# A fused attention and gated-MLP block: side tiles as single matmuls over the whole array, and a head ordered by traced load times

## The chip, the cores and the metric

One core of one Trainium2 chip. The metric is the device time of one launch in microseconds; the time of a kernel is the median of its runs. The engines are TensorE (matmul, weight load), VectorE, ScalarE, GpSimd and SyncE, which issues the DMAs.

## The reference

```python
x = A_x                                   # (1, 2048, 512), bf16
xn = layernorm(x)                         # no scale, no shift
q, k, v = split(xn @ wqkv)                # 32 heads of 16 columns
o = softmax(q @ k.T * 16 ** -0.5) @ v     # over all 2048 keys, for each head
h = silu(xn @ w1) * (xn @ w3)             # 1792 columns
return x + o @ wo + h @ w2
```

## The kernel before

The 2048 tokens are 16 token tiles of 128. The 32 heads are 8 groups of 4, so that the 4 heads of a group sit in the four strips of 32 partitions. A *unit* is a group and a block of queries (256 as a rule, 128 in the first two units and at the end).

Each score is computed twice. **Pass one** (line 1008) multiplies 128 queries by 512 keys for two heads at a time, in two strips of 32 rows of TensorE's array, and VectorE takes the row maxima of the two banks (line 1048, a TENSOR_REDUCE of 128x1024). Of these there are 1024. The maximum of a row goes, negated, into spare rows of the transposed queries (lines 1133 and 1135, and either a small matmul tile named AQ, or a DMA transpose). **Pass two** (line 1272) computes the scores again, keys on the partitions and the maximum already subtracted, and ScalarE takes the exponential into `PT` (line 1285, or 1315 for two banks at once). The tile named PV multiplies `PT` with the values and a column of ones; the sums of the ones are inverted on GpSimd and multiplied in by way of DMAs.

Everything else of TensorE is a **side tile** in a bank of its own: the K and Q of the first group straight into `KT` and `QT` (`tile_KT`, `tile_QT`), the others in `tile_heads` by way of a DRAM buffer, `tile_V`, the gate and up projections (`ffn_pair`, `G` and `U`), the output tiles (`tile_OUT`, `tile_OUTA`, `tile_OUTB`) and AQ. All of these and PV go through `col_groups` (line 564), which splits each product into four matmuls of 32 stationary columns, side by side in the four column strips of the array:

```python
for i in range(n):
    ins = e.matmul(bank(bk)[32 * i:32 * i + m, c0 + a:c0 + b], make_lhsT(i),
                   rhs if (a, b) == (0, ncols) else rhs[:, a:b],
                   start=start, stop=stop, tile_position=(0, 32 * i), **kw)
```

**The head.** SyncE loads `x` in five pieces, the weights between and behind them (`LOADS`). For each token tile: statistics on VectorE (line 593) or, for two groups of tiles, on ScalarE (583 and 587); coefficients on GpSimd (606, and the power at 609); the normalisation itself (line 626) on the engine that a letter of `NORM` names for its group, `d` VectorE, `p` GpSimd, `a` ScalarE (line 622); four transposes on TensorE (650); an eviction into `xnT` on ScalarE (657). When four token tiles are there, a K tile gives 512 keys of the first group.

```python
LN_GROUPS = ((0, 2), (2, 4), (4, 6), (6, 8), (8, 12), (12, 14), (14, 16))
NORM = "ddddppa"
```

In the first microseconds TensorE also runs **spare matmuls** on a tile of ones (`warm_cand`), later on `ident` and `xnT` (`fill_cand`), whose results nobody reads: they are there to keep TensorE's clock up.

**The order.** The order of each engine is written out when the program is built: a planner goes through all engines, with costs in microseconds for each instruction (`_c_mm`, `_c_act`, `_c_dve`), the landing times of the loads (`DMA_FIRST`, `DMA_RATE`), the costs of a change between row and column strips on TensorE (`pe_start`), and a running measure of how many columns TensorE has streamed lately (`note_load`), and picks for each engine the instruction that can start first. The chip then runs these fixed orders, with semaphores between the engines.

Of the kernel before, what the change touches and what calls it, by code (L numbers as in the profile page):

```python
# [14 lines left out]
_VIS = {"dve": 0.138, "pool": 0.085}  # L15

# [20 lines left out]
class _Prog:  # L37
# [87 lines left out]
    def pe_start(self, mode, groups, ready):  # L125
        t = max(self.free["pe"], ready)
        if mode == "col":
            t = max(t, max(self.rg) + (0.092 if self.pe_mode == "row" else 0.0))
        else:
            t = max(t, max(self.rg[g] for g in groups))  # L130
            if self.pe_mode == "col":
                t = max(t, max(self.rg) + 0.106)
        return t

    def pe(self, fn, reads, writes, mode, groups, dur, name="", first=None):
# [11 lines left out]
        for g in (range(4) if mode == "col" else groups):  # L147
            self.rg[g] = start + dur
        if mode == "row" and self.pe_mode == "col":
            for g in range(4):  # L150
                self.rg[g] = max(self.rg[g], start)
# [64 lines left out]
class _Tile:  # L216
    __slots__ = ("groups", "evac", "name", "bank", "pred", "need", "on_start", "paced", "cols")
# [29 lines left out]
def _build(nc, A_x, A_wqkv, A_wo, B_w1, B_w3, B_w2, out):  # L247
# [36 lines left out]
    DMA_FIRST = 3.25  # L284
# [34 lines left out]
    NORM = "ddddppa"  # L319
# [25 lines left out]
    with ctx:  # L345
# [134 lines left out]
        landed = [DMA_FIRST]  # L480

        def load(fn, keys, kb):
            landed[0] += kb / DMA_RATE
# [6 lines left out]
        def load_w(dst, keys, off, n=D):  # L490
            load(lambda e: e.dma_start(dst, wqkv_v[:, :, off * D:off * D + n]), keys, n if n == D else 280)
# [81 lines left out]

        def ln_chunk(gi):
# [43 lines left out]
            def norm(op):  # L618
                for t in tl:
# [11 lines left out]
                    else:  # L631
                        poolq["nx"].append(_Item(*it, 0.7, 0.8, **kw))
# [50 lines left out]
        def tile_heads(what, g0, ng, sc, need):  # L683
# [4 lines left out]
            def grp(c):  # L688
                return lambda bk: col_groups(bk, lambda i: w[:, c, 64 * g0 + 32 * i:64 * g0 + 32 * i + 32],
                                             lambda i: xnT[:, c, sc * 512:(sc + 1) * 512], 512,  # L690
                                             start=c == 0, stop=c == DC - 1, n=2 * ng)
# [43 lines left out]
        def tile_V(t, need=None):  # L735
            groups = []
            for c in range(DC):
                groups.append((lambda bk, c=c: col_groups(
                    bk, lambda i: xnT[:, c, t * 128 + 32 * i:t * 128 + 32 * i + 32], lambda i: wv[:, c, :], D,
# [12 lines left out]
        def qt_groups(qc, g, q0, nq, stop_last):  # L752
            groups = []
            for c in range(DC):
                groups.append((lambda bk, c=c: col_groups(
                    bk, lambda i: wpad["q", g][:, c, 32 * i:32 * i + 32],
                    lambda i: xnT[:, c, qc * 512 + q0:qc * 512 + q0 + nq], nq,
# [12 lines left out]
        def tile_QT2(u):  # L770
# [4 lines left out]
            for qt in range(nq // 128):  # L775
                groups.append((lambda bk, qt=qt: col_groups(
                    bk, lambda i: Z[:, par, qt, 32 * i:32 * i + 32], lambda i: ident[:, :], 128, c0=qt * 128,
                    start=False, stop=True, skip=True),
# [17 lines left out]
        def ffn_pair(sc, fc):  # L796
# [19 lines left out]
            def groups(which):  # L816
                return [(lambda bk, c=c: col_groups(
                    bk, lambda i: w13[:, sl, which * DC + c, 32 * i:32 * i + 32],
                    lambda i: xnT[:, c, sc * 512:(sc + 1) * 512], 512, start=c == 0, stop=c == DC - 1),
# [36 lines left out]
        def g_x(tg, stop=False):  # L856
            return (lambda bk: col_groups(bk, lambda i: ident[:, 32 * i:32 * i + 32], lambda i: xr[:, tg % NXR, :], D,
                                          start=True, stop=False),
                    [("ident",), ("xr", tg % NXR)], _c_mm(512), None)

        def g_h(tg, fc, stop=False):
            qc, ts = divmod(tg, 4)
            hs = hslot(qc * FC + fc)
            return (lambda bk: col_groups(bk, lambda i: hT[:, hs, ts * 128 + 32 * i:ts * 128 + 32 * i + 32],
                                          lambda i: w2[:, fc, :], D, start=False, stop=stop),
                    [("hT", hs), ("w2",)], _c_mm(512), None)

        def g_on(qc, ts, g, start, stop):
            ob = (qc + 1) % 2
            return (lambda bk: col_groups(bk, lambda i: onorm[ob][:, g, ts * 128 + 32 * i:ts * 128 + 32 * i + 32],  # L870
                                          lambda i: wo[:, g, :], D, start=start, stop=stop),
# [671 lines left out]
        def col_cand():  # L1543
            best = None
            for t in sorted(active, key=rank):
# [9 lines left out]
                st = P.pe_start("col", None, P.ready("pe", reads, writes))  # L1555
# [8 lines left out]
            def emit_half():  # L1564
# [3 lines left out]
                P.pe(a, reads, writes, "col", None, _c_mm(256), name=t.name, first="act")  # L1568
# [4 lines left out]
            def emit():  # L1573
                g = t.groups.pop(0)
                P.pe(fn, reads, writes, "col", None, dur, name=t.name, first="act")
# [44 lines left out]
        def warm_cand():  # L1620
# [3 lines left out]
            for bk in (3, 2, 5, 4) if not p1_n[0] else (5, 4):  # L1624
# [3 lines left out]
                st = P.pe_start("col", None, P.ready("pe", [("ones_t",)], writes))  # L1628

                def emit():  # L1630
# [4 lines left out]
                return st, emit, _c_mm(128)  # L1635
            return None

        def fill_cand():
# [8 lines left out]
            for fb in fbs:  # L1647
                if fb in bank_tenant or fb in p2_busy:
                    continue
                s_ = P.pe_start("col", None, P.ready("pe", (), [("ps", fb)]))  # L1650
# [6 lines left out]
            def emit():  # L1657
                P.pe(col_groups(bk, lambda i: ident[:, 32 * i:32 * i + 32], lambda i: xnT[:, 0, 0:512], 512),
# [253 lines left out]
```

## Time and profile before

| | us |
|---|---|
| median of three runs | 1217.35 |
| the three runs | 1213.72, 1217.36, 1217.35 |
| the profiled execution | 1215.26 |
| its span, first to last instruction | 1213.5 |
| busy: VectorE, ScalarE, TensorE, GpSimd | 1180.8, 1168.3, 1155.1, 453.4 |
| mean granted clock of TensorE | 0.992 |

Matmuls are pipelined, so TensorE's busy time holds their latency as well and is no measure of how full it is. In the rows of a timeline stand the start, the time from the first start to the last end, the engine, the line, the operation, what it writes and reads, the count, and in brackets the idle time ahead of it and what ended that. "issue" is a wait for nothing that the profile shows. A row of windows has, for each engine in the order PE, PEld, DVE, ACT, POOL, the busy time and the count of instructions, then TensorE's granted clock, the share of the DMA engines and GB/s.

### The profile page before, as it was taken

What the parts mean: (1) busy time and instruction counts of PE and PEld (TensorE: products, weight loads), DVE (VectorE), ACT (ScalarE), POOL (GpSimd) and SP (SyncE); (2) the same over time, 40 slices, a digit from 0 to 9 for tenths busy, and PEclk for the clock granted to TensorE, in tenths of its full rate; (3) what the DMA queues carried; (4) which work ended last, traced back from release to release, by engine and by line L of the source; (5) the groups of instructions that cost most, each with busy time, mean ns of one, the idle gap of its engine ahead of it and who ended that gap; (6) DMA issues with size and microseconds to landing.
All of it is one profiled execution on the core that took longest, in us unless ns stands there. A gap on an engine that the chain in (4) does not pass through costs nothing.

```text
span 1213.5 us, 45673 instructions
## 1 busy us (share of the span) xinstructions
PE 1155.1 (95%) x20085; PEld 479.1 (39%) x20085; DVE 1180.8 (97%) x1083; ACT 1168.3 (96%) x2276; POOL 453.4 (37%) x862
## 2 busy tenths in 40 slices
PE   6999999999999999999999999999999999999998
PEld 4343333333333433333333433333333333345554
DVE  6799999999999999999999999999999999999995
ACT  5599999999999999999999999999999999999997
POOL 6315563553422256552221246552222225233220
PEclk9799999999999999999999999999999999999999
DMA  6322322222101122120101122210000111100000
GB/s 172 102 63 62 85 53 80 55 54 55 33 16 36 30 63 57 37 49 20 25 17 29 38 57 51 50 46 18 25 20 18 38 42 27 30 22 18 14 12 23
DMA packets 131298, 52.84 MB, mean 44 GB/s; under 512 B 100140, under 2 KB 131100, under 8 KB 131100
## 3 DMA queue, kind: packets, MB, share of 16 engines
q1 hardware_dynamic: 131100, 49.93, 16.3%
q8 instruction: 157, 2.57, 0.9%
q14 instruction: 41, 0.34, 0.1%
HBM read 38.86 MB, written 6.74 MB: 38 GB/s over the span
## 4 chain that ended last, share of the span: by engine, by line
ACT 40%; PE 35%; DVE 20%; issue 2%; POOL 1%; DMA 1%; SPq 0%; ACTq 0%
ACT PT L1285 30%; DVE part L1048 20%; PE ps L564 20%; PE ps L1272 10%; PE ps L1008 5%; ACT PT L1315 4%; ACT th L823 2%; ACT zg L825 1%; ACT ub L829 1%; ACT U L1380 1%; ACT kq L728 1%; POOL hT L626 1%; DMA PT<-in_A_x_dram 0%; PE ps L650 0%; POOL a L810 0%
## 5 line engine op out<-in xcount | busy, mean ns | idle before, releaser
L1048 DVE TENSOR_REDUCE part<-ps 128x2 f32<-128x1024 f32 x1024 | 1161.2, 1214 | 13.6 <-PE ps L1008 13.5
L1285 ACT ACTIVATE PT<-ps 128x512 bf16<-128x512 f32 x1796 | 941.9, 631 | 6.1 <-PE ps L1272 4.3
L1272 PE MATMUL ps<-QT,KT 32*128 32x256 bf16 (+1 forms) x4672 | 542.8, 259 | 6.5 <-ACT PT L1315 5.2
L1008 PE MATMUL ps<-KT,QT 32*128 32x512 bf16 x2048 | 403.0, 386 | 2.1 <-DVE part L1048 1.5
L1272 PEld LDWEIGHTS ps<-QT,KT 32*128 32x128 bf16 x4672 | 206.1, 92 | 237.0 <-issue 95.5
L564 PE MATMUL ps<-xnT,ident 128*32 128x512 bf16 (+1 forms) x2732 | 205.8, 354 | 17.6 <-ACT PT L1315 8.9
L1405 POOL TENSOR_TENSOR Rc<-Lc,mone 128x8 f32<-128x8 f32 (+1 forms) x70 | 105.9, 1513 | 276.0 <-DMA Lc<-U 276.0
L564 PE MATMUL ps<-PT,Vaug 128*17 128x256 bf16 (+1 forms) x4672 | 182.7, 261 | 5.9 <-ACT PT L1285 1.4
L564 PE MATMUL ps<-xnT,w 128*32 128x512 bf16 (+1 forms) x2304 | 156.3, 337 | 7.2 <-ACT zg L825 4.3
L1008 PEld LDWEIGHTS ps<-KT,QT 32*128 32x128 bf16 x2048 | 98.7, 91 | 125.6 <-issue 63.7
L1315 ACT ACTIVATE PT<-ps 128x1024 bf16<-128x1024 f32 x126 | 128.7, 1052 | 1.6 <-PE ps L1272 1.2
L564 PEld LDWEIGHTS ps<-PT,Vaug 128*17 128x17 bf16 x4672 | 87.7, 89 | 86.4 <-issue 56.4
L564 PEld LDWEIGHTS ps<-xnT,ident 128*32 128x32 bf16 x2732 | 53.9, 94 | 99.3 <-ACT PT L1285 45.2
L810 POOL TENSOR_TENSOR a<-zg,ub 128x512 f32<-128x512 bf16 x56 | 64.7, 1155 | 51.3 <-ACT ub L829 51.1
L564 PEld LDWEIGHTS ps<-xnT,w 128*32 128x32 bf16 x2304 | 46.2, 94 | 81.4 <-issue 48.5
L564 PE MATMUL ps<-w,hT 128*32 128x512 bf16 (+1 forms) x1116 | 72.2, 341 | 0.0
L812 POOL TENSOR_TENSOR hT<-a,t 128x512 bf16<-128x512 f32 x56 | 71.2, 1272 | 2.1
L1156 POOL TENSOR_TENSOR mx<-part 128x16 f32<-128x16 f32 (+1 forms) x62 | 13.2, 212 | 132.3 <-DVE part L1048 132.2
L1425 POOL TENSOR_TENSOR wk_on<-U,R 128x256 bf16<-128x256 f32 (+1 forms) x37 | 23.4, 633 | 97.1 <-DMA R<-rd 97.1
L1425 POOL TENSOR_TENSOR on_b<-U,R 128x256 bf16<-128x256 f32 (+1 forms) x33 | 23.5, 713 | 79.6 <-DMA R<-rd 79.5
L807 POOL TENSOR_SCALAR t<-th 128x512 f32<-128x512 bf16 x56 | 34.8, 621 | 13.2 <-ACT th L823 10.0
L829 ACT ACTIVATE ub<-ps 128x512 bf16<-128x512 f32 x56 | 36.2, 647 | 1.3 <-PE ps L564 1.3
(89 smaller groups left out, 541.6 us busy)
## 6 DMA issues: line engine op xcount, KB each, us to landing
w<-in_B_w_dram SPq DMA_DIRECT2D x112, 128.0 KB
R<-rd SPq DMA_DIRECT2D x55, 128.0 KB
QT<-qd SPq DMA_DIRECT2D x31, 128.0 KB
KT<-kd SPq DMA_DIRECT2D x28, 128.0 KB
xr<-in_A_x_dram SPq DMA_DIRECT2D x16, 128.0 KB
out_dram<-osb SPq DMA_DIRECT2D x16, 128.0 KB
qd<-kq SPq DMA_DIRECT2D x15, 128.0 KB
w<-in_B_w_dram SPq DMA_DIRECT2D x1, 1792.0 KB
```

What stands on the lines that cost most here:

```text
L564: ins = e.matmul(bank(bk)[32 * i:32 * i + m, c0 + a:c0 + b], make_lhsT(i), rhs if (a, b) == (0, ncols) else rhs[:, a:b], start=start, stop ...
L807: q.append(_Item(lambda e: e.tensor_scalar(t1[:, :], th[:, ss, :], 1.0, 1.0, ALU.mult, ALU.add), [("th", ss)], [("t1",)] + ([("st", t) for ...
L810: q.append(_Item(lambda e: e.tensor_tensor(a32[:, :], zg[:, ss, :], ub[:, ss, :], ALU.mult), [("zg", ss), ("ub", ss)], [("a32",)], 1.1, 1.25))
L812: q.append(_Item(lambda e: e.tensor_tensor(hT[:, hslot(idx), :], a32[:, :], t1[:, :], ALU.mult), [("a32",), ("t1",)], [("hT", hslot(idx))] ...
L829: return [_Item(lambda e: e.activation(ub[:, ss, :], bank(bk), ACTF.Identity), [("ps", bk)], [("ub", ss)], _c_act(512), cb=part_done)]
L1008: ins = e.matmul(bank(2 * sl + i), QT[32 * j:32 * j + 32, qs, q * 128:(q + 1) * 128], KT[32 * j:32 * j + 32, g, c_ * 512:(c_ + 1) * 512], ...
L1048: redq.append(_Item(lambda e: e.tensor_reduce(dst, pair_ap.rearrange("p (a b) -> p a b", b=512), AX.X, ALU.max), writes, [("part", par, qt ...
L1272: ins = e.matmul(bank(b)[:, i * nq:(i + 1) * nq], KT[32 * j:32 * j + 32, g, (k0 + i) * 128:(k0 + i + 1) * 128], QT[32 * j:32 * j + 32, qs, ...
L1285: expq.append(_Item(lambda e: e.activation(PT[:, sl, :], bank(b), ACTF.Exp, scale=SCALE), [("ps", b)], [("PT", sl)], _c_act(512), cb=cb, e ...
L1315: return _Item(lambda e: e.activation(PT[:, s0:s1 + 1:s1 - s0, :], ps8[:, b0:b1 + 1, :], ACTF.Exp, scale=SCALE), [("ps", b0), ("ps", b1)], ...
L1405: poolq["nrm"].append(_Item(lambda e: e.tensor_tensor(Rc[:, pp, 0:nl], Lc[:, pp, 0:nl], mone[:, 0:nl], ALU.pow), [("Lc", pp), ("mone",)], ...
L1425: poolq["nrm"].append(_Item(lambda e: e.tensor_tensor(onorm[ob][:, g, q0:q0 + nq], U[:, us, 0:nq], R[:, pp, 0:nq], ALU.mult), [("U", us)] ...
```

## The change

Side tiles and spare matmuls go through a new helper, `all_groups`: one matmul of up to 128 stationary columns over the whole array, where four of 32 stood. PV stays with `col_groups`. A spare matmul on ones has 512 columns, or 128 where only that fits, where it had 128. In the head a spare matmul of 128 columns may now stand where a longer one doesn't fit. `NORM` changes: token tiles 8 to 11 go from GpSimd to VectorE, 12 and 13 from GpSimd to ScalarE. The planner gets costs for the third array mode, and landing times of the loads in three stages. The orders of all engines are computed anew with these, so they differ throughout; the numbers of instructions on ScalarE, VectorE, GpSimd and SyncE are the same but for the normalisation and two pairs of exponentials that are taken singly.

```diff
+_SWITCH = {("row", "col"): 0.092, ("row", "all"): 0.092, ("col", "all"): 0.1, ("all", "col"): 0.1}
...
-        if mode == "col":
-            t = max(t, max(self.rg) + (0.092 if self.pe_mode == "row" else 0.0))
+        if mode != "row":
+            t = max(t, max(self.rg) + (_SWITCH.get((self.pe_mode, mode), 0.0)))
...
+        self.mode = "col" if name.startswith("PV") else "all"
...
-    DMA_FIRST = 3.25
+    DMA_FIRST = 2.95
...
-    NORM = "ddddppa"
+    NORM = "dddddaa"
...
-            landed[0] += kb / DMA_RATE
+            kb_sum[0] += kb
+            landed[0] += kb / (DMA_RATE if kb_sum[0] <= 512 or kb_sum[0] > 1792 else 170.0 if kb_sum[0] <= 1024
+                               else 255.0)
...
+        def all_groups(bk, lhsT, rhs, ncols, c0=0, start=True, stop=True, rows=128, skip=False):
+            def part(a, b, start, skip):
+                def f(e):
+                    kw = dict(skip_group_check=True) if skip else {}
+                    return e.matmul(bank(bk)[0:rows, c0 + a:c0 + b], lhsT,
+                                    rhs if (a, b) == (0, ncols) else rhs[:, a:b], start=start, stop=stop, **kw)
+                return f
+            f = part(0, ncols, start, skip or ncols == 512)
+            if ncols == 512:
+                f.halves = part(0, 256, start, True), part(256, 512, False, True)
+            return f
...
-                groups.append((lambda bk, c=c: col_groups(
-                    bk, lambda i: wpad["k", 0][:, c, 32 * i:32 * i + 32],
-                    lambda i: xnT[:, c, sc * 512:(sc + 1) * 512], 512, start=c == 0, stop=c == DC - 1),
+                groups.append((lambda bk, c=c: all_groups(
+                    bk, wpad["k", 0][:, c, :], xnT[:, c, sc * 512:(sc + 1) * 512], 512,
+                    start=c == 0, stop=c == DC - 1),
...
-                    P.pe(col_groups(bk, lambda i: ones_t[:, 32 * i:32 * i + 32], lambda i: ones_t[:, :], 128),
-                         [("ones_t",)], writes, "col", None, _c_mm(128), name="fill")
-                    note_load(st, 512)
+                    P.pe(all_groups(bk, ones_t[:, :], ones_t[:, :].unsqueeze(1).broadcast_to([128, n, 128]), 128 * n),
+                         [("ones_t",)], writes, "all", None, _c_mm(128 * n), name="fill")
+                    note_load(st, 512 * n)
...
+                    elif f[0] + _c_mm(128) <= c[0] + 0.03 and P.free["pe"] < WARM_FILL:
+                        c = (f[0], f[3], _c_mm(128))
```

The other side tiles change as the K tile does.

More of the change, by code (lines that the diff above doesn't have):

```diff
@@ L146, in pe @@
             dur = 2 * dur
-        for g in (range(4) if mode == "col" else groups):
+        for g in (range(4) if mode != "row" else groups):
             self.rg[g] = start + dur
-        if mode == "row" and self.pe_mode == "col":
+        if mode == "row" and self.pe_mode != "row":
             for g in range(4):
@@ L490, in load_w @@
         def load_w(dst, keys, off, n=D):
-            load(lambda e: e.dma_start(dst, wqkv_v[:, :, off * D:off * D + n]), keys, n if n == D else 280)
+            load(lambda e: e.dma_start(dst, wqkv_v[:, :, off * D:off * D + n]), keys, n if n == D else 64)
         for what in LOADS:
@@ L1574, in emit @@
                 g = t.groups.pop(0)
-                P.pe(fn, reads, writes, "col", None, dur, name=t.name, first="act")
+                P.pe(fn, reads, writes, t.mode, None, dur, name=t.name, first="act")
                 if t.paced:
@@ L1657, in emit @@
             def emit():
-                P.pe(col_groups(bk, lambda i: ident[:, 32 * i:32 * i + 32], lambda i: xnT[:, 0, 0:512], 512),
-                     [("ident",)] + xnT_keys(0, 512), writes, "col", None, _c_mm(512), name="fill")
+                P.pe(all_groups(bk, ident[:, :], xnT[:, 0, 0:512], 512),
+                     [("ident",)] + xnT_keys(0, 512), writes, "all", None, _c_mm(512), name="fill")
                 note_load(st, 2048)
@@ L1663, in emit_half @@
             def emit_half():
[L1664 to L1665 removed]
+                P.pe(all_groups(bk, ident[:, :], xnT[:, 0, 0:256], 256),
+                     [("ident",)] + xnT_keys(0, 256), writes, "all", None, _c_mm(256), name="fill")
                 note_load(st, 1024)
```

63 lines of the change are left out of this document (30 added, 33 removed).

## The prediction

> **What bounds the kernel now.** I read the page first: the busy shares, then the costliest groups.
>
> ```profile
> span 1213.5 us, 45673 instructions
> PE 1155.1 (95%) x20085; PEld 479.1 (39%) x20085; DVE 1180.8 (97%) x1083; ACT 1168.3 (96%) x2276; POOL 453.4 (37%) x862
> ...
> L1048 DVE TENSOR_REDUCE part<-ps 128x2 f32<-128x1024 f32 x1024 | 1161.2, 1214 | 13.6 <-PE ps L1008 13.5
> ```
>
> VectorE is busy for 97% of the span, and 1161.2 of its 1180.8 us are the 1024 row maxima, 1161.2 / 1024 = 1.134 us each. They had to wait for TensorE for 13.5 us in all. The question is where, so I read the windows next, and then VectorE's timeline.
>
> ```profile
> 15.00:20.00 5.00, 3.08 (x42) 2.02 (x46) 0.68 (x3) 0.72 (x2) 4.89 (x3) 0.66 0.90 193
> ...
> 35.00:40.00 5.00, 5.00 (x44) 1.73 (x42) 3.58 (x3) 1.62 (x4) 0.00 (x0) 0.50 0.01 2
> ...
> 200.00:300.00 100.00, 98.44 (x1484) 39.31 (x1484) 100.00 (x90) 100.00 (x207) 46.36 (x82) 1.00 0.24 59
> ```
>
> ```profile
> 15.52 0.17 DVE L596 BATCH_NORM_AGGREGATE mv<-t 128x2 f32<-128x6 f32 x1
> 21.64 1.23 DVE L1048 TENSOR_REDUCE part<-ps 128x2 f32<-128x1024 f32 x1 [5.96 <-PE ps L1008]
> ...
> 22.87 4.90 DVE L1048 TENSOR_REDUCE part<-ps 128x2 f32<-128x1024 f32 x4
> 29.27 0.16 DVE L614 SCALAR_TENSOR_TENSOR lnb<-mv,lnr 128x2 f32<-128x2 f32 x1 [1.50 <-POOL lnr L609]
> ...
> 32.96 1.23 DVE L1048 TENSOR_REDUCE part<-ps 128x2 f32<-128x1024 f32 x1 [2.40 <-PE ps L1008]
> 35.44 2.36 DVE L1048 TENSOR_REDUCE part<-ps 128x2 f32<-128x1024 f32 x2 [1.25 <-PE ps L1008]
> 38.26 1.23 DVE L1048 TENSOR_REDUCE part<-ps 128x2 f32<-128x1024 f32 x1 [0.46 <-PE ps L1008]
> 40.43 1.23 DVE L1048 TENSOR_REDUCE part<-ps 128x2 f32<-128x1024 f32 x1 [0.95 <-PE ps L1008]
> 42.58 1.23 DVE L1048 TENSOR_REDUCE part<-ps 128x2 f32<-128x1024 f32 x1 [0.93 <-PE ps L1008]
> 44.30 4.69 DVE L1048 TENSOR_REDUCE part<-ps 128x2 f32<-128x1024 f32 x4 [0.49 <-PE ps L1008]
> ...
> 82.31 28.37 DVE L1048 TENSOR_REDUCE part<-ps 128x2 f32<-128x1024 f32 x25 [1.06 <-PE ps L1008]
> ...
> 1192.39 0.17 DVE L1185 TENSOR_REDUCE negm<-part 128x4 f32<-128x16 f32 x1
> ```
>
> Only 12 of the 1024 maxima are done by 44.30 us (1+4 by 27.8, then 1+1+2+1+1+1). The other 1012 take from 44.30 to 1192.39, 1148.1 us, which is 1.134 us each: back to back, with one gap of 1.06 at 82. So behind 44.30 the kernel runs at VectorE's rate, with ScalarE as full beside it (100.00 of 100 in the window 200 to 300), and the last 21 us are a tail that the change leaves alone. What can be won lies ahead of 44.30: the waits there sum to 5.96+1.50+2.40+1.25+0.46+0.95+0.93+0.49 = 13.94 us.
>
> Two causes show in the timelines of TensorE and GpSimd.
>
> ```profile
> 11.88 1.24 PE L564 MATMUL ps<-ones_t 128*32 128x128 bf16 x74
> ...
> 16.91 0.61 PE L564 MATMUL ps<-ones_t 128*32 128x128 bf16 x14 [3.80 <-issue]
> ...
> 17.22 3.28 PE L564 MATMUL ps<-xnT,wk_on 128*32 128x512 bf16 x32
> ...
> 15.92 4.15 POOL L626 TENSOR_SCALAR hT<-PT,mv,lnr 128x512 bf16<-128x512 bf16 x2
> ...
> 31.46 0.59 PE L650 MATMUL ps<-ident,hT 128*128 128x128 bf16 x4 [2.16 <-POOL hT L626]
> ```
>
> ```profile
> L626 POOL TENSOR_SCALAR hT<-PT,mv,lnr 128x512 bf16<-128x512 bf16 x6 | 12.4, 2078 | 0.3
> ...
> L626 DVE TENSOR_SCALAR hT<-PT,mv,lnr 128x512 bf16<-128x512 bf16 x8 | 3.1, 426 | 0.1
> ```
>
> First, TensorE stood still for 3.80 us in the middle of its spare matmuls and waited for nothing that the profile names; it had run 350 pairs of weight load and matmul by then. It came back at a clock of 0.66, so that the first K and Q tiles (the 32 matmuls) took 3.28 us. Second, a token tile costs 2.078 us on GpSimd against 0.39 (3.1 / 8) on VectorE, six of them 12.4 us in a row, and TensorE's transposes wait for them; the clock is at 0.50 from 35 to 40.
>
> **The change part by part.**
>
> *Spare matmuls and side tiles as single matmuls.* Four matmuls of 32 columns become one of 128. In the changed program's order TensorE runs 49 pairs up to the first K tile, where it ran 365. If the stall of 3.80 us is the feed of the instructions, it has no cause left there, and the half clock behind it goes too. I take it so: the stall sits where the DMA share is 0.90, and 350 small pairs ahead of it are most of what TensorE had been given. In the steady part the count falls from 20085 matmuls to about 14100, which buys nothing, since VectorE is full. What must be costed is whether a single is dearer than four.
>
> ```profile
> 20.43 0.84 PE L650 MATMUL ps<-ident,hT 128*128 128x128 bf16 x12
> ...
> L650 PEld LDWEIGHTS ps<-ident,hT 128*128 128x128 bf16 x64 | 4.2, 106 | 7.6 <-ACT hT L622 2.3 <-DVE hT L626 1.5 <-ACT xnT L657 1.5
> ...
> L564 PEld LDWEIGHTS ps<-xnT,ident 128*32 128x32 bf16 x2732 | 53.9, 94 | 99.3 <-ACT PT L1285 45.2 <-ACT PT L1315 21.9 <-DVE part L1048 10.7
> ```
>
> The transposes are the one whole-array form in the trace. Twelve take 0.84 us; less the 0.22 of the last, one comes every 0.056 us, its weight load of 0.106 included, so the load is hidden behind the matmul ahead of it. A single should thus cost its columns and no more, like the four it replaces. From below, it may save the steps between the four; from above, if no load were hidden, it costs 0.106 more. I take nought, as the transposes are the nearest row. The Trainium skill, "TensorE: Matmul & The Clock Gate", Part 3 (What overlaps and what doesn't), says that a weight load overlaps a running matmul only when its row group differs. Under it each single would pay its load in full; by that rule the time is that of the third rival below, and the twelve transposes speak against it.
>
> ```profile
> 24.79 0.39 PE L1008 MATMUL ps<-KT,QT 32*128 32x512 bf16 x2
> ...
> 25.11 0.10 PEld L564 LDWEIGHTS ps<-xnT,wk_on 128*32 128x32 bf16 x4 [0.23 <-issue]
> ```
>
> The weighted values keep the column form, so there are now three modes. A change of mode costs about 0.1 us: 0.32 from the score pair's start to the next load, less 512 columns, which the row above of 32 matmuls bounds at 0.41 a group at half clock, so about 0.21 at full. Counted in the two orders, changes go from 2557 to 2610: 53 x 0.1 = 5 us of TensorE over the whole run. They hide behind the spare matmuls that the order holds anyway (under rival two I price their loss of cover).
>
> *Normalisation off GpSimd.* Four of its six tiles go to VectorE, 4 x 0.39 = 1.55 us on the bounding engine, ahead of the first maximum; two more go to ScalarE, which waits there. The 1.50 us wait for GpSimd's coefficients and the transposes' waits for 2 us tiles go.
>
> *The order from the traced load times.* In the new order the first two normalisations stand ahead of the statistics of tile 4, where VectorE idles:
>
> ```profile
> 7.34 0.69 DVE L593 BATCH_NORM_STATS2 t<-PT 128x6 f32<-128x512 bf16 x1 [1.01 <-DMA PT<-in_A_x_dram]
> ...
> 14.80 1.01 POOL L609 TENSOR_TENSOR lnr<-lnt,mhalf 128x4 f32<-128x4 f32 x1
> ```
>
> That fills 1.01 us. VectorE's head work then ends at 15.69 - 1.01 + 1.55 + 0.1 = 16.3 us; the coefficients of tiles 8 to 11 came at 15.81 and come up to 1.0 earlier with their statistics, at 14.8, plus four normalisations 16.4. So the first maximum can start at 16.4 in place of 21.64, and go on if TensorE delivers.
>
> *The sum.* Waits gone 13.94, gap filled 1.01, work added 1.55: 13.4 at best. What is late next is the K tile of the last 512 keys, whose tokens 14 and 15 need a coefficient after the seventh maximum (24.3), ScalarE's two normalisations, transposes, evictions and a tile among ScalarE's other work; I work that out as 31 to 32 us from rows of about 0.6 each, and the fifteenth maximum would ask for it at 16.4 + 14 x 1.134 = 32.3. That is tight, so I keep 1.5 us of waits: 11.9 us gained, with 8.4 if the chain comes 5 late. ScalarE must move as far:
>
> ```profile
> 0.00:51.40 51.40, 39.67 (x751) 20.51 (x751) 34.07 (x56) 24.89 (x50) 24.40 (x39) 0.83 0.42 117
> ...
> 51.45 1.09 ACT L1285 ACTIVATE PT<-ps 128x512 bf16<-128x512 f32 x2 [0.51 <-PE ps L1272]
> ```
>
> Its first exponential waits for the sixteenth maximum; ahead of it ScalarE is busy for 24.89 of 51.4 us, so it has room to start 12 us earlier, with some 1.5 us of normalisation more. Behind that its work is the same but for two pairs of exponentials fewer.
>
> So the span goes to 1213.5 - 11.9 = 1201.6. The profiled execution took 1215.26, 1.76 more than its span, and the median of the three is 1217.35; taken from that, **1205.4 us**.
>
> **The rivals.** *One: the stall stays.* It may belong to the time (the bulk loads) and not to the count of instructions. Then the first maximum still starts at about 21.6, and only the later waits go, 7.98 less 1.5: a gain of 6.5, 1210.9 us. For it: the DMA share. Against it: the stall falls amid the small matmuls.
>
> *Two: slower, by the clock.* The gate may count a single as less work than four. At 0.50 the maxima at 38.26, 40.43 and 42.58 stand 2.16 apart in place of 1.134, a loss of 1.02 each. It decides from 11.7 maxima on, 25 us at half clock. With 60 us of it, 28 maxima, the loss is 28.5: 1217.35 - 11.9 + 28.5 = 1234. The spare matmuls' cover for the mode changes would be lost with it, 5 us more at most. The Trainium skill, same page, Part 1, lets the clock fall only after an idle window of about 3.4 us; by that rule this rival has no chance where no such gap is. The trace shows 0.50 from 35 us on, where the longest gap behind the 3.80 is 2.16 us, so I leave it one.
>
> *Three: the loads show.* About 2010 singles at 0.106 are 213 us more of TensorE, which idles 58 us (1213.5 - 1155.1): about 155 lost, 1360 us.
>
> *Four: given back.* VectorE meets some 12 us of new waits among its 1012 maxima, as the one of 1.06 at 82: no change.
>
> **How the numbers follow.** The forecast (9 to 13.4 gained) 0.70, rival one 0.14, two 0.08, three 0.02, four 0.06. A measurement of this kernel cannot tell less than 0.3%, 3.7 us. So faster 0.84, same 0.06, slower 0.10. The range: the best sum gives 1204.0, and the fastest run before lies 3.6 below its median, 1200.4; upwards it takes in rival one and 1 us: 1212. It leaves out rivals two to four, 0.16.
>
> **What the changed profile would show.** Right: no wait on "issue" of over 1 us in TensorE's first 20 us; clock 1.0 in the windows from 10 to 45; the first maximum near 16 to 18, at least 22 maxima by 44 us, the first exponential near 39; VectorE at 100 in the windows behind. Wrong: the stall at another place, a maximum waiting for TensorE for over 3 us between 25 and 35 (the last K tile), a clock under 0.9 behind 50 us, or new waits in the maxima's row above the 13.6 of now.

## The result and the profile after

| | before | after |
|---|---|---|
| median, us | 1215.85 (4 runs, 1213.72 to 1217.36) | 1202.29 (4 runs, 1201.7 to 1203.5) |
| the profiled execution, us | 1215.26 | 1202.28 |
| its span, us | 1213.5 | 1200.4 |
| mean granted clock of TensorE | 0.992 | 0.996 |

The ratio is 0.9891, 95% interval 0.987 to 0.9912: 1.1% faster. Timed a second time beside other kernels (six runs, below) it was 0.9914, 0.989 to 0.9938. The forecast was 1205.4, range 1200.4 to 1212.0. Two executions below lie far outside and do not enter the ratios: 1500.08 of the first experiment, at a mean clock of 0.568, and 2897.85 of the kernel before, timed beside it.

The page of the kernel after: the span, the busy shares, the queue that brings the engines their instructions (packets, MB, share), and the maxima.

```profile
span 1200.4 us, 32683 instructions
PE 1124.1 (94%) x13504; PEld 466.0 (39%) x13660; DVE 1181.3 (98%) x1088; ACT 1169.9 (97%) x2280; POOL 439.3 (37%) x856
...
q8 instruction: 107, 1.75, 0.6%
...
L1062 DVE TENSOR_REDUCE part<-ps 128x2 f32<-128x1024 f32 x1024 | 1160.2, 1207 | 1.5 <-PE ps L1286 0.7
```

The maxima wait 1.5 us in all, where they waited 13.6. TensorE issues a third fewer pairs of weight load and matmul (13660 weight loads in place of 20085; 156 matmul records are missing in this trace). VectorE's timeline tells where those 1.5 us lie:

```profile
6.88 0.73 DVE L643 TENSOR_SCALAR hT<-PT,mv,lnr 128x512 bf16<-128x512 bf16 x2 [0.31 <-POOL lnr L626]
...
16.13 2.32 DVE L1062 TENSOR_REDUCE part<-ps 128x2 f32<-128x1024 f32 x2
...
18.43 5.84 DVE L1062 TENSOR_REDUCE part<-ps 128x2 f32<-128x1024 f32 x5
...
24.46 10.26 DVE L1062 TENSOR_REDUCE part<-ps 128x2 f32<-128x1024 f32 x9
...
37.31 17.05 DVE L1062 TENSOR_REDUCE part<-ps 128x2 f32<-128x1024 f32 x15
...
54.37 509.19 DVE L1062 TENSOR_REDUCE part<-ps 128x2 f32<-128x1024 f32 x450
563.80 1.23 DVE L1062 TENSOR_REDUCE part<-ps 128x2 f32<-128x1024 f32 x1 [0.24 <-PE ps L1286]
565.52 1.23 DVE L1062 TENSOR_REDUCE part<-ps 128x2 f32<-128x1024 f32 x1 [0.50 <-PE ps L1286]
567.39 548.17 DVE L1062 TENSOR_REDUCE part<-ps 128x2 f32<-128x1024 f32 x484 [0.64 <-PE ps L1022]
...
1178.35 0.17 DVE L1199 TENSOR_REDUCE negm<-part 128x4 f32<-128x16 f32 x1
```

The first maximum starts at 16.13 in place of 21.64, and from there to 563 no maximum has a bracket with a wait. The three brackets near 565 sum to 1.38 us. The last reduction stands at 1178.35 in place of 1192.39, 14.04 earlier; the tail behind it takes 22.05 in place of 21.11, so the span is 13.1 shorter.

TensorE's head, in its timeline: no wait on "issue", the first K and Q tiles in 1.89 us in place of 3.28.

```profile
2.40 5.22 PE L583 MATMUL ps<-ones_t 128*128 128x512 bf16 x12
...
9.18 1.67 PE L583 MATMUL ps<-ones_t 128*128 128x512 bf16 x7
10.69 1.89 PE L583 MATMUL ps<-xnT,wk_on 128*128 128x512 bf16 x8
...
13.81 0.40 PE L1022 MATMUL ps<-KT,QT 32*128 32x512 bf16 x4 [0.47 <-ACT QT L780]
```

The windows (last three columns: clock, DMA share, GB/s) hold full clock through the head, in every window of 5 us up to 60. The lowest behind it is 500 to 600, with the dip that the three brackets belong to.

```profile
15.00:20.00 5.00, 4.36 (x38) 2.40 (x37) 5.00 (x11) 5.00 (x12) 0.89 (x2) 1.00 0.95 198
...
35.00:40.00 5.00, 4.68 (x52) 2.30 (x51) 4.97 (x6) 4.30 (x10) 4.82 (x6) 1.00 0.69 190
...
500.00:600.00 100.00, 92.56 (x1027) 35.08 (x1039) 98.51 (x88) 98.46 (x186) 37.52 (x73) 0.97 0.13 32
```

### The profile page after: what moved, and what is told of

Same layout as the page of the kernel before. It is cut to its first block, busy times and chain, and to the rows that moved or that the text cites. A ratio compares the mean times of both kernels' runs of the same rounds, so it can differ in the third digit from the quotient of the medians.

```text
span 1200.4 us, 32683 instructions
## 1 busy us (share of the span) xinstructions
PE 1124.1 (94%) x13504; PEld 466.0 (39%) x13660; DVE 1181.3 (98%) x1088; ACT 1169.9 (97%) x2280; POOL 439.3 (37%) x856
## 4 chain that ended last, share of the span: by engine, by line
ACT 38%; PE 34%; DVE 25%; issue 2%; DMA 0%; POOL 0%; ACTq 0%; another core or an unknown queue 0%
ACT PT L1299 29%; DVE part L1062 23%; PE ps L583 13%; PE ps L1286 10%; PE ps L569 6%; ACT PT L1329 5%; PE ps L1022 5%; ACT th L838 1%; ACT zg L840 1%; ACT U L1394 1%; ACT ub L844 1%; ACT kq L745 1%; DVE t L610 1%; DVE hT L643 0%; ACT Vaug L760 0%
## 5 line engine op out<-in xcount | busy, mean ns | idle before, releaser
L1062 DVE TENSOR_REDUCE part<-ps 128x2 f32<-128x1024 f32 x1024 | 1160.2, 1207 | 1.5 <-PE ps L1286 0.7
L1286 PE MATMUL ps<-QT,KT 32*128 32x256 bf16 (+1 forms) x4672 | 549.4, 259 | 9.9 <-ACT PT L1329 4.3
L583 PE MATMUL ps<-xnT,ident 128*128 128x512 bf16 (+1 forms) x565 | 167.4, 350 | 25.0 <-ACT PT L1329 9.8
L583 PE MATMUL ps<-xnT,w 128*128 128x512 bf16 (+1 forms) x538 | 145.9, 337 | 11.6 <-ACT zg L840 5.0
L583 PEld LDWEIGHTS ps<-xnT,ident 128*128 128x128 bf16 x652 | 48.1, 96 | 106.6 <-ACT PT L1299 54.2
L583 PEld LDWEIGHTS ps<-xnT,w 128*128 128x128 bf16 x566 | 43.1, 97 | 80.4 <-issue 47.4
L583 PE MATMUL ps<-w,hT 128*128 128x256 bf16 (+1 forms) x266 | 68.3, 338 | 2.1 <-issue 1.3
L1170 POOL TENSOR_TENSOR mx<-part 128x16 f32<-128x16 f32 (+1 forms) x62 | 13.1, 211 | 152.6 <-DVE part L1062 152.5
L822 POOL TENSOR_SCALAR t<-th 128x512 f32<-128x512 bf16 x56 | 34.7, 619 | 11.5 <-ACT th L838 9.4
L838 ACT ACTIVATE th<-ps 128x512 bf16<-128x512 f32 x56 | 36.0, 642 | 2.3 <-PE ps L583 2.3
```

The source lines that it names most:

```text
L583: return e.matmul(bank(bk)[0:rows, c0 + a:c0 + b], lhsT, rhs if (a, b) == (0, ncols) else rhs[:, a:b], start=start, stop=stop, **kw)
L838: return [_Item(lambda e: e.activation(th[:, ss, :], bank(bk), ACTF.Tanh, scale=0.5), [("ps", bk)], [("th", ss)], _c_act(512), cb=part_don ...
L1062: redq.append(_Item(lambda e: e.tensor_reduce(dst, pair_ap.rearrange("p (a b) -> p a b", b=512), AX.X, ALU.max), writes, [("part", par, qt ...
L1286: ins = e.matmul(bank(b)[:, i * nq:(i + 1) * nq], KT[32 * j:32 * j + 32, g, (k0 + i) * 128:(k0 + i + 1) * 128], QT[32 * j:32 * j + 32, qs, ...
```

## The experiments

My theory at the start was that of the prediction: the stall is the feed of TensorE's instructions and goes with their number; the waits behind it go because GpSimd's slow tiles go. The rivals were that the stall belongs to the loads, that the waits come from something else in the order, and that singles weaken the clock. Each kernel below is named by the edit, and computes the whole reference. Medians are over 4 to 10 runs. They come from three timings, two on one chip and one on another; the kernel before took 1216.52, 1216.32 and 1216.0 in them.

**Spare matmuls single, nothing else.**

```diff
 # before, in warm_cand
-P.pe(col_groups(bk, lambda i: ones_t[:, 32 * i:32 * i + 32], lambda i: ones_t[:, :], 128),
+P.pe(lambda e: e.matmul(bank(bk)[:, 0:128], ones_t[:, :], ones_t[:, :], start=True, stop=True),
```

> The kernel before, its order unchanged, but each group of four spare matmuls in the head is one matmul over the whole array, still of 128 columns; 110 pairs of weight load and matmul stand ahead of the first K tile, where 365 stood. Theory (the stall of 3.80 us is the feed of the instructions): no wait on issue of over 1 us ahead of the K tile, clock 1.0 from 15 to 20 us, first maximum near 16 to 18 us in place of 21.64, a gain of 4 to 6 us: 1210 to 1213 us. Rival (the stall belongs to the time, with the bulk loads): TensorE still stands still from about 13 to 17 us, and the time is that of before, 1216.

Measured: 1213.35, ratio 0.9973 (0.9959 to 0.9987), a gain of 3.2 where 4 to 6 was expected. VectorE's timeline:

```profile
16.29 1.23 DVE L1048 TENSOR_REDUCE part<-ps 128x2 f32<-128x1024 f32 x1 [0.47 <-PE ps L1008]
...
23.76 1.23 DVE L1048 TENSOR_REDUCE part<-ps 128x2 f32<-128x1024 f32 x1 [2.32 <-PE ps L1008]
...
30.20 1.23 DVE L1048 TENSOR_REDUCE part<-ps 128x2 f32<-128x1024 f32 x1 [2.39 <-PE ps L1008]
...
41.46 4.69 DVE L1048 TENSOR_REDUCE part<-ps 128x2 f32<-128x1024 f32 x4 [0.41 <-PE ps L1008]
```

The stall is gone (TensorE has no wait on "issue" at all in this trace) and the first maximum comes 5.35 earlier, but the fifth waits 2.32 and others behind it as well; by the row at 41.46 twelve are done, as by 44.30 in the kernel before. Of 5.35 us 2.84 are left: the maxima ran into the late token tiles, with the clock at 0.50 from 25 to 40.

**The spare matmuls of the head in strips again, in the order after.** `all_groups` for the tile of ones becomes four matmuls of 32 columns for each 128.

```diff
 # after, in warm_cand
-P.pe(all_groups(bk, ones_t[:, :], ones_t[:, :].unsqueeze(1).broadcast_to([128, n, 128]), 128 * n),
-     [("ones_t",)], writes, "all", None, _c_mm(128 * n), name="fill")
+def f(e):
+    for m in range(n):
+        for i in range(4):
+            ins = e.matmul(bank(bk)[32 * i:32 * i + 32, 128 * m:128 * m + 128],
+                           ones_t[:, 32 * i:32 * i + 32], ones_t[:, :], start=True, stop=True,
+                           tile_position=(0, 32 * i))
+    return ins
+P.pe(f, [("ones_t",)], writes, "all", None, _c_mm(128 * n), name="fill")
```

> The changed kernel, but each spare matmul on ones in the head is cut into pieces of 32 stationary and 128 moving columns, as before; the planned order is the same, and 353 pairs stand ahead of the first K tile, where 49 stood. Theory (feed of the instructions): a wait on issue of 2 to 4 us comes back near 13 us, the clock falls below 0.8 there, the first maximum moves from 16.1 to about 20 us, and the time is 1205 to 1208. Rival (the stall belongs to something else that the change took away, as the order of the loads' use): no stall, 1202.

Measured: 1211.3, ratio 0.9964 (0.9945 to 0.9982). TensorE's timeline:

```profile
10.88 0.29 PE L1648 MATMUL ps<-ones_t 128*32 128x128 bf16 x6 [2.18 <-issue]
...
12.41 2.70 PE L1648 MATMUL ps<-ones_t 128*32 128x128 bf16 x110
17.46 0.23 PE L1648 MATMUL ps<-ones_t 128*32 128x128 bf16 x2 [2.35 <-issue]
17.62 3.38 PE L583 MATMUL ps<-xnT,wk_on 128*128 128x512 bf16 x8
```

The stall is back, twice, and costs 9 us, more than I expected: the first maximum is 6.2 later, and a wait of 1.50 follows. It stands behind the 223rd and the 351st pair of weight load and matmul. Those are the places in the kernel before too, where I had seen only the second:

```profile
10.33 0.57 PE L564 MATMUL ps<-ones_t 128*32 128x128 bf16 x26 [0.76 <-issue]
```

**The bulk loads later**, in the kernel before: the residual tiles and the first MLP weights are issued only behind the first Q tile.

```diff
 # before
+            late = (lambda: ("QT", 0) in done) if idx < 2 else None
-                      [], [("w13", sl, 0)])
+                      [], [("w13", sl, 0)], pred=late)
...
-                      cb=lambda op: done.add(("xr", tg)))
+                      cb=lambda op: done.add(("xr", tg)), pred=(lambda: ("QT", 0) in done) if tg < NXR else None)
```

> The kernel before, but the loads of the first two residual tiles and of the first two pairs of MLP weights (0.8 MB) are issued only once the first Q tile is planned to be there; the order of TensorE, VectorE and ScalarE is unchanged. Theory with the bulk loads as the reason why the instructions come late: 0.8 MB at some 350 GB/s is 2.3 us, so the stall ends 2 us earlier, at 1 to 2 us in place of 3.80, and the time is 1212 to 1215. Theory with the count alone: the stall stays at 3.8 us, 1216.

Measured: 1215.09, ratio 0.9987 (0.9973 to 1.0001), between the two expectations, and a gain is not shown. TensorE's timeline:

```profile
11.70 0.93 PE L565 MATMUL ps<-ones_t 128*32 128x128 bf16 x26 [2.12 <-issue]
...
14.30 2.62 PE L565 MATMUL ps<-ones_t 128*32 128x128 bf16 x88
```

One stall of 2.12 at the 223rd pair; the 351st runs through among the 88, at about 16.2. So the places are set by the count. What the length goes with is seen in the view of the DMA queues. In the kernel before, three packets of instructions came in the first 20 us; in the kernel after, one:

```profile
q8 instruction: 3, 0.05, 1.0%
```

```profile
q8 instruction: 1, 0.02, 0.4%
```

On the page of before the queue moved 157 packets, 2.57 MB, 16.4 KB each. The 20085 pairs are 40170 instructions, 256 for each packet; in the kernel after 13660 pairs come to 255 for each of 107. The second of the three, in the kernel before, stands in the window 14.0 to 14.5:

```profile
q8 instruction: 1, 0.02, 14.3%
```

In windows of that size it lies at 15.0 to 15.5 with the small spares in the order after, and at 14.0 to 14.5 in each of the two kernels of "each half alone" below. TensorE goes on behind the 351st pair at 16.91 (before), 17.46, 17.08 and 16.65, which is 2.0 to 3.1 us later. With the loads moved it lies at 13.5 to 14.0, over 2 us ahead of the need. Counted from where TensorE went on behind the 223rd pair, the packet's window begins 3.7 to 4.1 us later in the four kernels with the loads in place and 1.8 later in this one. The distance of 128 pairs is 256 instructions. The Trainium skill, "Runtime: NRT & Kernel Launch" (Instruction fetch mechanics), says that an engine's instructions are refilled in blocks of 16 KiB, 256 instructions, and that crossing a block is mostly hidden. Size and distance agree here; hidden it was not, with 0.76 + 3.80 us in the kernel before. It was hidden in the first experiment, where the 223rd pair comes only behind 23 us, 8 us behind the first packet (15.0 to 15.5). That a packet which comes late makes the stall is read from places and times in five kernels. That the loads make it late rests on this one run, whose time hardly moved, and two things in it speak against so simple a reading. Its first packet, ahead of any load that was moved, came a microsecond later than in the kernel before (8.5 to 9.0 in place of 7.5 to 8.0), so a packet's time varies without these loads; and the DMA share was still 1.00 to 1.13 between 11.5 and 14. So why a packet is late stays open.

**GpSimd normalises again, in the order after.**

```diff
 # after
-    NORM = "dddddaa"
+    NORM = "ddddppa"
```

> The changed kernel with the six normalisations back on GpSimd (priced at the traced 2.08 us each). Theory as predicted (the transposes wait for the 2 us tiles): VectorE waits for TensorE between 25 and 45 us by about 4 to 8 us, less the 1.55 us of normalisation that it is spared: 1205 to 1209 us. Rival (with the stall gone and an order that knows the price, the tiles come in time: six of them end at about 28 us, while 16 maxima of the first 1024 keys last until 33): no wait, VectorE 1.5 us shorter, 1200 to 1202 us.

Measured: 1201.97, ratio 0.9896 (0.9857 to 0.9935), no slower than the change. No maximum waits for a GpSimd tile:

```profile
14.87 1.19 DVE L1062 TENSOR_REDUCE part<-ps 128x2 f32<-128x1024 f32 x1
...
16.06 8.10 DVE L1062 TENSOR_REDUCE part<-ps 128x2 f32<-128x1024 f32 x7
```

The first comes 1.26 earlier than after, since VectorE has four normalisations less to do. So GpSimd's slowness was not what made the maxima wait, and that half of my theory fell. For these tiles the two kernels differ in one thing more, the planner's price of a tile on GpSimd, 2.08 in place of 0.7: a line of the diff not shown above, and without use in the change itself, where GpSimd normalises nothing.

**That price alone, with single spares**, on the kernel before:

```diff
 # before, and the edit of the first experiment
-                        poolq["nx"].append(_Item(*it, 0.7, 0.8, **kw))
+                        poolq["nx"].append(_Item(*it, 2.08, 2.2, **kw))
```

> The kernel with single spare matmuls of the first experiment (everything else as before), in which the planner now prices a normalisation on GpSimd at the traced 2.08 us in place of 0.7; the six stay on GpSimd. Theory formed on the run with the six back on GpSimd (what cost the head its second half was an order that expected the tiles too early, so that TensorE's queue stood before their transposes): no wait of VectorE of over 1 us between 16 and 45 us, 1200 to 1204 us. Rival (the slow engine itself, or the planner's old load times, or the side tiles' form): the waits of VectorE between 20 and 45 us stay at 5 us or more, 1208 to 1213 us.

Measured: 1203.01, ratio 0.9892 (0.9862 to 0.9923). That is the whole gain, with strips in the side tiles, the old load times and six tiles on GpSimd, until 30.2 us. The clock stays at 1.00 from 10 to 45 us, where the kernel before had 0.50 to 0.62 between 30 and 45:

```profile
24.00 6.20 POOL L626 TENSOR_SCALAR hT<-PT,mv,lnr 128x512 bf16<-128x512 bf16 x3
```

```profile
15.83 1.23 DVE L1048 TENSOR_REDUCE part<-ps 128x2 f32<-128x1024 f32 x1 [0.42 <-PE ps L1008]
...
17.06 8.24 DVE L1048 TENSOR_REDUCE part<-ps 128x2 f32<-128x1024 f32 x7
...
31.59 6.88 DVE L1048 TENSOR_REDUCE part<-ps 128x2 f32<-128x1024 f32 x6 [0.19 <-PE ps L1008]
```

TensorE works in a fixed order. When the planner takes a tile for 0.7 us, it puts its transposes early, and the score pairs queued behind them wait with them, as the 2.16 us at 31.46 in the prediction's rows, where the 13th token tile is transposed behind 6 score pairs. With 2.08 it stands behind 11, and waits for nothing (with the 12th, in one row):

```profile
27.55 0.62 PE L650 MATMUL ps<-ident,hT 128*128 128x128 bf16 x8
```

**Each half alone.** The price alone, and the letters of `NORM` alone, both on the kernel before, with its spares in strips.

```diff
 # before: the price alone
-                        poolq["nx"].append(_Item(*it, 0.7, 0.8, **kw))
+                        poolq["nx"].append(_Item(*it, 2.08, 2.2, **kw))
```

> The kernel before with the planner's price of a normalisation on GpSimd at 2.08 us in place of 0.7, and nothing else; the spare matmuls stay cut in four. Theory (two halves that are needed together: the stall of TensorE's instructions, and an order that knows when the late token tiles come): the stall of 3 to 4 us near 17 us stays, the first maximum waits for TensorE and starts at 21.5 to 22.5, and behind it no maximum waits over 1 us: 1207 to 1210. Rival (the price alone carries the gain, the stall being idle time that another wait would fill): first maximum near 16 to 18, 1202 to 1205. Second rival (GpSimd's 2 us tiles themselves hold the maxima up): waits of 1 to 2.4 us between 25 and 45 stay, 1213 to 1216.

```diff
 # before: the letters alone
-    NORM = "ddddppa"
+    NORM = "dddddaa"
```

> The kernel before, with the new assignment of the normalisations alone (four to VectorE, two to ScalarE); spare matmuls and side tiles in strips, old load times. Theory: the stall of 3.8 us at the 351st pair stays and with it a first maximum after 20 us, but the waits behind it go: 1208 to 1212 us. Rival (both halves are needed, one alone gains next to nothing): 1214 to 1216.

Measured: price 1208.94, ratio 0.9943 (0.9928 to 0.9957); letters 1207.8, ratio 0.9923 (0.9901 to 0.9945), just below the 1208 to 1212 expected. First the price, then the letters:

```profile
21.97 1.23 DVE L1048 TENSOR_REDUCE part<-ps 128x2 f32<-128x1024 f32 x1 [6.92 <-PE ps L1008]
...
23.20 8.24 DVE L1048 TENSOR_REDUCE part<-ps 128x2 f32<-128x1024 f32 x7
```

```profile
22.41 1.23 DVE L1048 TENSOR_REDUCE part<-ps 128x2 f32<-128x1024 f32 x1 [6.35 <-PE ps L1008]
...
27.41 13.66 DVE L1048 TENSOR_REDUCE part<-ps 128x2 f32<-128x1024 f32 x12
```

In both the stall stays, the first maximum waits for it, and the waits behind are gone. By the medians the price alone gives 7.1, single spares alone 3.2, both 13.3: together 3.1 more than their sum, because without the price the late tiles eat what the stall gives up.

**Side tiles in strips, in the order after.** `all_groups` issues four matmuls of 32 columns; the spares stay single (their three calls pass `strips=False`).

```diff
 # after, in all_groups
-        def all_groups(bk, lhsT, rhs, ncols, c0=0, start=True, stop=True, rows=128, skip=False):
+        def all_groups(bk, lhsT, rhs, ncols, c0=0, start=True, stop=True, rows=128, skip=False, strips=True):
...
-                    return e.matmul(bank(bk)[0:rows, c0 + a:c0 + b], lhsT,
-                                    rhs if (a, b) == (0, ncols) else rhs[:, a:b], start=start, stop=stop, **kw)
+                    if not strips:
+                        return e.matmul(bank(bk)[0:rows, c0 + a:c0 + b], lhsT,
+                                        rhs if (a, b) == (0, ncols) else rhs[:, a:b], start=start, stop=stop, **kw)
+                    for i in range(rows // 32):
+                        ins = e.matmul(bank(bk)[32 * i:32 * i + 32, c0 + a:c0 + b], lhsT[:, 32 * i:32 * i + 32],
+                                       rhs if (a, b) == (0, ncols) else rhs[:, a:b], start=start, stop=stop,
+                                       tile_position=(0, 32 * i), **kw)
+                    return ins
```

> The changed kernel in its own order, but each side tile's single matmul is emitted as four strips of 32 stationary columns again (the spare matmuls stay single, and the planner's costs stay). Theory as predicted (a single costs its columns, as the four do; VectorE is the bound): within 2 us of the changed kernel, 1201 to 1204 us, unless the instruction feed of the first 40 us stalls again at pairs 223 or 351, which now lie at about 20 to 28 us, with the loads over by then. Rival (singles are cheaper on TensorE and that mattered): 1206 or more, with new waits of the maxima for TensorE behind 50 us.

Measured: 1209.79, ratio 0.9946 (0.9927 to 0.9964), a miss: 7.5 us lost. The head is sound (first maximum 16.61). The loss is spread:

```profile
L1068 DVE TENSOR_REDUCE part<-ps 128x2 f32<-128x1024 f32 x1024 | 1164.9, 1215 | 3.2 <-PE ps L1292 0.9
```

The row holds 4.7 us more than after, with 1.7 more of waits. A maximum by itself takes 1.23, in a run 1.134, so 4.7 would be the overlap lost by some 49 maxima (an estimate, 4.7 / 0.096) whose scores came just too late. The instructions' feed is not it: the longest wait on "issue" is 0.3 in both kernels. In this order, then, four strips are dearer than one single. Whether by steps between the strips or by changes of mode between them and the single spares, which the planner here takes as free, isn't settled. The kernel with the price and single spares, whose order is planned with strips, does not lose it.

**The old load times, in the order after.**

```diff
 # after
-    DMA_FIRST = 2.95
+    DMA_FIRST = 3.25
...
-            landed[0] += kb / (DMA_RATE if kb_sum[0] <= 512 or kb_sum[0] > 1792 else 170.0 if kb_sum[0] <= 1024
-                               else 255.0)
+            landed[0] += kb / DMA_RATE
...
-            load(lambda e: e.dma_start(dst, wqkv_v[:, :, off * D:off * D + n]), keys, n if n == D else 64)
+            load(lambda e: e.dma_start(dst, wqkv_v[:, :, off * D:off * D + n]), keys, n if n == D else 280)
```

> The changed kernel with the load times of before in the planner (first load at 3.25 us, one rate, the small column load counted as 280 KB). Theory (the load times only set whether VectorE normalises ahead of the statistics of tile 4): the gap of about 1 us on VectorE near 7 us is back, the first maximum starts near 17, no long waits behind it: 1 us slower than the changed kernel, 1202.5 to 1204.5. Rival (the order as a whole hangs on the load times): waits of over 2 us among the first 24 maxima, 1206 to 1211.

Measured: 1203.61, ratio 0.9901 (0.9884 to 0.9918). VectorE waits for the load of tile 4 with the statistics ahead of the normalisations, as before:

```profile
7.93 0.70 DVE L609 BATCH_NORM_STATS2 t<-PT 128x6 f32<-128x512 bf16 x1 [1.45 <-DMA PT<-in_A_x_dram]
...
17.21 1.23 DVE L1061 TENSOR_REDUCE part<-ps 128x2 f32<-128x1024 f32 x1 [1.02 <-PE ps L1021]
```

The first maximum is 1.08 later than after and nothing waits long behind it. The medians differ by 1.3, with intervals that overlap.

**Spares over a quarter of the array, in the steady part**, to try the clock.

```diff
 # after, in fill_cand (and so for 256 columns)
-                P.pe(all_groups(bk, ident[:, :], xnT[:, 0, 0:512], 512),
+                P.pe(col_groups(bk, lambda i: ident[:, 0:32], lambda i: xnT[:, 0, 0:512], 512, n=1),
```

> The changed kernel, but the spare matmuls behind the head (on ident and xnT, 465 of 512 and 187 of 256 columns) cover one strip of 32 stationary columns in place of 128: the same count and the same time on TensorE, a quarter of the array. It asks what the clock counts. If it counts the time that the array is busy, nothing changes: clock 0.99 or more, 1202 us. If it counts how much of the array works, the clock falls in many windows, to a mean below 0.97, VectorE waits for TensorE there, and the time is 1210 to 1240 us.

Measured: 1207.37, ratio 0.9917 (0.9887 to 0.9947), between the two expectations. The mean clocks of its four runs are 0.989 to 1.0, no lower than those of the kernel after (0.987 to 0.999 in ten runs); its time at clock 1.0 was 1203.23. So in these four runs a quarter of the area shows no lower clock. Why the run at 1.0 is 2.7 slower than the change at 0.999 (1200.52, below) stays open.

**The change and its best variant, side by side.**

> The changed kernel with GpSimd normalising the two groups that it normalised before, as in the earlier run of it, now timed side by side with the changed kernel. VectorE has 1.55 us less to do ahead of its first maximum. If that counts it is 1 to 3 us faster than the changed kernel (1199.5 to 1201.5); if the maxima behind set the end as they did in the first timing, the two agree within 1 us.

> The changed kernel itself, unedited, beside the one with GpSimd's normalisation on the same chip: 1201.5 to 1203.5 as before, and a clock dip of 5 to 10 us in the steady part if the dip near 560 us belongs to its order.

Measured: with GpSimd normalising 1199.88, ratio 0.9873 (0.9858 to 0.9888); the change itself 1205.49, ratio 0.9914 (0.989 to 0.9938), above the 1201.5 to 1203.5 expected, its six runs from 1200.52 to 1210.74. The spread follows the clock. Over all ten runs of the change, a mean clock of 0.999 went with 1200.52, 0.996 with 1202.15 and 1202.28, 0.991 with 1207.2, 0.987 with 1210.74: 0.85 us for each 0.001 (10.22 / 12). In the profiled one of the six the clock is full at 565. One dip lies around 300, a longer one begins near 1129:

```profile
300.00:310.00 10.00, 9.91 (x110) 3.28 (x107) 8.16 (x8) 7.97 (x15) 1.89 (x3) 0.69 0.07 16
...
1125.00:1130.00 5.00, 4.66 (x111) 2.90 (x111) 4.86 (x7) 4.86 (x12) 0.88 (x3) 0.88 0.09 17
1130.00:1135.00 5.00, 5.00 (x45) 2.28 (x43) 3.53 (x3) 3.40 (x5) 1.01 (x1) 0.50 0.04 4
```

So the dip is not tied to the order. At a mean clock of 0.998 or more the variant ran in 1199.17 to 1200.16 (five runs of its eight), the change in 1200.52 to 1202.3 (three of ten). The variant beats the kernel before. Against the change it is 1.0 to 1.4 faster at a clock of 0.999 (1199.17 and 1199.49 against 1200.52), as the 1.26 at the first maximum would have it, and level at 0.995 (1203.65 against 1203.5 and 1203.79); more is not shown. Most of the 5.6 between the two medians goes with the clock, with dips that fell on one and not on the other.

## Why the prediction was right, and where it was not

**The place and the sum held.** Nearly all of the gain lies ahead of 44.30, and the sum closes: 13.4 at best, as worked out, plus 1.06 for the wait at 82 that is gone too, plus 1.0 because longer runs of maxima overlap more (1161.2 to 1160.2), less 1.38 at the dip, less 0.94 for the tail, is 13.1, the difference of the spans. Of the signs, the first maximum was put at 16.4 and came at 16.13; "at least 22 maxima by 44 us" are 23; no "issue" wait stands in the first 20 us; the first exponential, put near 39, starts at 36.79. One sign of the other kind did show, a clock under 0.9 behind 50 us; it cost 1.38.

**Two terms were mis-sized.** The 1.5 us of residual waits in the head are nought. The last K tile was put at 31 to 32, and its eviction ends at 31.00, the early end; the fifteenth maximum starts at about 32.4 (24.46 + 7 x 1.134) and finds it there:

```profile
30.31 0.69 ACT L690 ACTIVATE KT<-ps,kbias 128x512 bf16<-128x512 f32 x1 [0.69 <-PE ps L583]
```

And the tail, said to be left alone, grew by 0.94. Of the 3.1 us between forecast and result the span makes 1.2 (1201.6 against 1200.4); the other 2 are the base, a median of three of 1217.35 that lay 2.1 above the profiled execution, where the later medians are 1216.0 to 1216.5.

**The stall** was rightly put down to the instructions, and rival one (the loads) may be half right: with the loads moved the second packet came 2 us sooner behind the first stall (1.8 in place of 3.7 to 4.1), for a reason that stays open. The prediction took the number for the cause without knowing the unit; the 365 pairs ahead of the first K tile cross the edges at 223 and 351, the 41 of the changed order (49 with the eight of the first K and Q tiles) none.

**The second step had the right edit and the wrong reason.** "Normalisation off GpSimd" takes the waits of 25 to 44 away: the letters alone do it. But the reason given, that TensorE waits because such a tile takes 2 us, is not enough: with its true price the planner finds an order in which six such tiles delay no maximum. The waits came from an order worked out with a false price, and the letters help by using only engines whose price is nearer (0.34 on VectorE, traced at 0.39; 0.71 on ScalarE, traced at some 0.8). So the 7.98 us of later waits went as forecast, but not for the reason given, and in that the number had luck. As a way to that end the move is the dearer one: it costs 1.26 us at the first maximum (the estimate was 1.55).

**A single at the price of four** held for the head: eight in 1.89 us, less the 0.39 of the last, is 0.214 each, its weight load of 0.096 hidden. In the first experiment the same tiles in 32 strips took 1.91 at full clock:

```profile
12.82 1.91 PE L564 MATMUL ps<-xnT,wk_on 128*32 128x512 bf16 x32
```

The weight loads of the singles, in the kernel after:

```profile
L583 PEld LDWEIGHTS ps<-xnT,ident 128*128 128x128 bf16 x652 | 48.1, 96 | 106.6 <-ACT PT L1299 54.2 <-ACT PT L1329 23.5 <-DVE part L1062 8.4
```

That is rival three refuted, and with it, for this form, the rule that it rested on. The mode changes stayed under VectorE's cover, as said. Rival two, the clock, is not what the change does, but its mechanism was seen: 0.85 us per 0.001 of mean clock, 2.4 us at half clock, is 0.35 lost per us at half clock, where the prediction had 1.02 / 2.16 = 0.47. Its "0.50 from 35 us on" begins sooner, at a clock of 0.51 in the window from 30 to 35. Rival four did not come.

## What to carry to other kernels

When a static order makes engines wait for one that is late, look first whether the planner's price of its instruction is the one in the trace: here one number (2.08 for 0.7) and the single spares were worth as much as the whole change. Count instructions in the head of a kernel, spare ones too: many small ones, used up faster than their packets arrive, can starve the engine that they were to keep warm. And two causes that follow each other in time can each be worth little alone and their sum and more together, so undo them one at a time from both ends.

## What the runs showed of the hardware

TensorE's instructions come in packets of 16.4 KB over the same DMA engines as the data, one for each 256 of its instructions, and the two edges seen here lie 128 pairs of weight load and matmul apart. Where the pairs were small it stood there for 0.32 to 3.80 us.

The granted clock fell to 0.50 in the steady part, for some 7 us in one execution of the change and for up to some 20 in another, in other places of the same program. Ahead of the dip at 565, from 540 us on, TensorE's longest gaps are 0.41 and 0.68 us. In the kernel with the loads moved it was 0.50 from 11.5 to 14, behind the stall of 2.12. The Trainium skill, "TensorE: Matmul & The Clock Gate", Part 1 (A second HAM failure mode), tells of a clock that swings where TensorE idles often and briefly between groups of matmuls; the gaps here fit that better than the single idle window of 3.4 us cited in the prediction. What starts a dip, and how to keep them away, stays open.
